# Loads of k and v for the last two batches: k through SyncE's queue, v through GpSimd's, fewer and larger issues for batch 18

## The chip, the cores and the metric

The kernel runs on one core of a Trainium2 chip. The metric is the device time of one execution in microseconds (us); the median of three runs before the change is 207.99 us (207.58 to 208.32).

## What is computed

The reference chains two parts. The first is a recurrence over the sequence, per batch and head; the second is a feed-forward network with squared ReLU on its output.

```python
# q, k, v: [4 batches, 8 heads, 768 steps, 64]; gamma[h] = 1 - 2**(-5-h); scale = 1/8
for t in range(768):
    state = gamma * state + outer(k[:, :, t], v[:, :, t])      # [4, 8, 64, 64]
    y[:, :, t] = scale * q[:, :, t] @ state
x = y laid out as [3072 tokens, 512]
h = maximum(x @ w_in, 0)          # w_in  [512, 2048]
out = (h * h) @ w_out             # w_out [2048, 512], out float32
```

## The kernel before, in words

**Chunks and blocks.** The recurrence is computed in chunks of 128 steps: six chunks for each of four batches, numbered 0 to 23. Chunks 6 to 11, 12 to 17 and 18 to 23 are the second, third and fourth batch. For each chunk TensorE (PE) makes scores (k against q), which VectorE masks, the state (k against v, added up over the chunks of a batch), and outputs (v against the masked scores, plus the state against q). The outputs become x of the feed-forward part. Its work goes in blocks of four chunks and then of two; the second matrix product is done with seven products of half size in place of eight, from sums that VectorE prepares.

**Where the order comes from.** The order is written out by hand. The feed-forward part is a list of pieces of TensorE work; the place number n counts them, from 4 upward. `put(place, what, ...)` hangs a step of the recurrence, a load or a store in front of that place. So the program order on every engine, and on SyncE's and GpSimd's queues, follows from the places, and each engine takes its instructions in that order. A chunk takes eight places in the later part of the kernel, which is about 7.5 us of TensorE's time.

**The half form (chunks 8 to 23), `attend2`.** The chunk's last step, the outputs, has place d. In front of it stand, for an even chunk, the scaling of q by VectorE (`scale_q`, two steps) and a transpose of q by a DMA on SyncE's queue (`dma_transpose_q`, L425); for every chunk

- `cast_k2` (L658): GpSimd casts k from the staged float32 tile into `ks_bdp`, in two halves of 64 partitions; there are two such tiles, taken in turn;
- `transpose_k2` (L681): a transposing DMA on SyncE's queue writes `kT` from `ks_bdp`; there are two kT tiles;
- `scale_v2`: VectorE scales v by the table `kf2` (L667), and GpSimd copies the result into `v_bd`, in two halves (L675);
- `scores2` (L697, five places ahead of d): TensorE multiplies kT with the transposed q, and VectorE masks (L704);
- `state2` (L724) and `outputs2` (L746, L753).

For chunks 12 to 23, k is cast at d - 18, transposed at d - 13, and v scaled and copied at d - 9. d is 57, 62, and then 70, 78, 86 and so on.

**Loads of q.** One load on SyncE's queue brings q for two chunks (512 KB, L105).

**Loads of k and v for the half form, `batch_loads`.** It is a generator: each `next` issues one load (L147) of some chunks of one head's k or v into 64 partitions of a staged tile. Four pairs of heads and two halves make eight issues for a group of chunks. Batch "8" (chunks 8 to 11, the last four of the second batch) is loaded four chunks at a time on SyncE's queue, batch 12 (chunks 12 to 17) and batch 18 (18 to 23) three at a time on GpSimd's queue. `places` says at which place each issue stands. The first half of batch 12's k goes into a tile that held sums of the feed-forward part.

**Other steps around it.** `pack_constants` makes lng2, a mask and, in its second step, the table `kf2` (two VectorE operations, L202 and L203, and one on ScalarE, L284); the steps stand at places 22 and 38. The stores of the feed-forward part (L886, L888) go through SyncE's queue too.

Of the kernel before, what the change touches and what calls it, by code (L numbers as in the profile page):

```python
# [28 lines left out]
def kernel(  # L29
# [9 lines left out]
    nc = tc.nc  # L39
# [87 lines left out]
    def stage_tile(size):  # L127
        t = stage.tile([P, 2 * NCH * NPAIR * D], FP32, name="stage")
        return t[:, 0:size]
# [3 lines left out]
    def batch_loads(m, name, size):  # L133


        b, i = chunks[m]
        src, to = (k, raw_k) if name == "k" else (v, raw_v)
        t = kept_tiles.pop((m, name), None)
        if t is None:
            t = stage_tile(2 * NCH * NPAIR * D)  # L140
        t = t.rearrange("s (p w d) -> s p w d", p=NPAIR, d=D)
        for j in range(NCH - i):
            to[m + j] = t[:, :, 2 * j : 2 * j + 2].rearrange("s p u d -> s u p d")
        for w in range(0, NCH - i, size):
            for hh, rows in enumerate(halves):
                for p in range(NPAIR):
                    (nc.sync if m == 8 else nc.gpsimd).dma_start(  # L147
                        t[rows, p, 2 * w : 2 * (w + size)],
                        src[b, 2 * p + hh, (i + w) * C : (i + w + size) * C].rearrange(
                            "(w s) d -> s w d", s=64  # L150
                        ),
                    )
                    yield
# [110 lines left out]
    def pack_constants():  # L264
        lng2 = const.tile([P, 2, NPAIR], FP32)
        for hh, rows in enumerate(halves):
            for p in range(NPAIR):
                nc.gpsimd.memset(lng2[rows, :, p : p + 1], float(np.log(gammas[2 * p + hh])))
        logs = lng2.rearrange("s u p -> s (u p)")
        scaled = exponents([[C, NCH], [C // 2, 2], [0, NPAIR]], 1, "ex_k2", logs, halves)  # L270
        nc.gpsimd.memset(cmask2[:], 0.0)
        for rows in halves:
            nc.gpsimd.affine_select(
                out=cmask2[rows],
                in_=cmask2[rows],
                compare_op=ALU.is_gt,
                fill=1.0,
                base=0,
                pattern=[[-1, 2], [-2, C // 4]],
                channel_multiplier=1,  # L280
            )
        yield
        ex = scaled()
        nc.scalar.activation(kf2.rearrange("s i u p -> s i (u p)"), ex[:], AF.Exp, scale=-1.0)  # L284
        yield
# [73 lines left out]
    at = {m: {} for m in range(NCHUNK)}  # L359
# [303 lines left out]
    def scale_v2(m):  # L663
        b, i = chunks[m]
        vn = raw_v.pop(m)
        v2 = v2pool.tile([P, 2 * NPAIR, D], BF16, name="v2")
        nc.vector.tensor_tensor(  # L667
            out=v2.rearrange("s (u p) d -> s u p d", u=2),
            in0=vn,
            in1=kf2[:, i, :, :, None].to_broadcast([P, 2, NPAIR, D]),  # L670
            op=ALU.mult,
        )
        v_bd = v_bd2s[m % 2]
        for hh, rows in enumerate(halves):
            nc.gpsimd.tensor_copy(v_bd[rows, :, hh, :], v2[rows])  # L675
        at[m].update(v2=v2, v_bd=v_bd)

    def transpose_k2(m):
        a = at[m]
# [535 lines left out]
    def put(place, what, *args):  # L1215
        parts.setdefault(place, []).append((what, args))
# [17 lines left out]
    def attend2(m, d, before, q_at, qturn_at, k_at, turn_at, v_at):  # L1234
        if m % 2 == 0:
            put(q_at, scale_q, m, 0)
            put(q_at + 1, scale_q, m, 1)
            put(qturn_at, dma_transpose_q, m)
        put(k_at, cast_k2, m)
        put(v_at, scale_v2, m)  # L1240
        put(turn_at, transpose_k2, m)
        put(max(d - 6, before), state2, m, 0)
        put(d - 5, scores2, m)
        put(d - 3, state2, m, 1)
        put(d, outputs2, m)
# [40 lines left out]
        put(place, early_store, tb, which)  # L1286
    packed = pack_constants()
    put(22, next, packed)
    put(38, next, packed)
    for j, t in enumerate(ks_bd2s + v_bd2s + [s_bds[2]]):  # L1290
        for hh in range(2):
            put(24 + j, zero_off_diagonal, t, hh)
# [7 lines left out]
    for m, d in zip(range(PACK_FROM, NCHUNK), done):  # L1300
        attend2(m, d, done[m - PACK_FROM - 1] if m > PACK_FROM else 0,
                *ahead.get(m, (d - 19, d - 16, d - 18, d - 13, d - 9)))
        if m >= 12 and m % 2 == 0:
            put(d - 33, load_q, m)
    places = {
        (8, "k"): [23, 23, 24, 24, 25, 32, 32, 33],
        (8, "v"): [33, 33, 34, 34, 35, 35, 36, 36],
        (12, "k"): [49, 50, 51, 52, 53, 54, 55, 56] + [74 + j for j in range(8)],
        (12, "v"): [58, 59, 60, 61, 62, 64, 65, 66] + [82 + j for j in range(8)],
        (18, "k"): [92 + 4 * j // 3 for j in range(8)] + [117 + 4 * j // 3 for j in range(8)],  # L1310
        (18, "v"): [103 + 4 * j // 3 for j in range(8)] + [128 + 4 * j // 3 for j in range(8)],
    }
    for (m, name), at_places in places.items():
        loads = batch_loads(m, name, 4 if m == 8 else 3)
        for place in at_places:
            put(place, next, loads)

# [53 lines left out]
```

## Time and profile before

| what | value |
|---|---|
| median of three runs | 207.99 us (207.58 to 208.32) |
| the profiled execution | 208.36 us, span 206.6 us |
| granted TensorE clock, mean | 0.998 |
| DMA queues | SyncE's: q1, hardware_dynamic; GpSimd's: q0, software_dynamic |
| k and v for batches 12 and 18 | 32 + 32 issues on GpSimd's queue, 96 KB each, 4.5 and 4.9 us median to landing |
| kT | 16 transposes on SyncE's queue, 4.9 us median to landing (3.1 to 9.5) |
| HBM | 27.26 MB read, 6.29 MB written |

The page gives, for each engine, busy time and its share of the span. PE is TensorE's matrix work, PEld its loading of weights, DVE is VectorE, ACT is ScalarE, POOL is GpSimd, SP is SyncE and SPq its queue of instructions. L147 is line 147 of the kernel. A group's line names what it writes and reads as out<-in, with buffer numbers left out. Waits are put down to what came last. The chain of waits goes back from the last instruction to what released it, step by step; its lines give a start, a duration and the work. "Issue to landing" of a DMA is from the start of its issue to the last of its completion marks.

### The profile page before, as it was taken

The numbers are of one execution on the slowest core, as the hardware profiler recorded it, in microseconds if no ns is written. First come the engines' busy times: TensorE is split into PE (matmuls) and PEld (weight loads), VectorE is DVE, ScalarE is ACT, GpSimd is POOL, SyncE is SP. The second block draws the span as 40 slices with busy tenths as digits, with TensorE's granted clock in tenths as the row PEclk, the third lists the DMA queues.
The fourth block names the chain that finished last, engine by engine and source line by source line (L and its number), as shares of the span: only waits on it lengthen the run. The fifth ranks groups of instructions, "written<-read, shape, count | busy, mean of one in ns | idle before, by whom it ended". The sixth has DMA issues, their size and how long they took to land.

```text
span 206.6 us, 5855 instructions
## 1 busy us (share of the span) xinstructions
PE 196.7 (95%) x2373; PEld 165.2 (80%) x2373; DVE 152.9 (74%) x305; ACT 135.6 (66%) x276; POOL 112.1 (54%) x198
## 2 busy tenths in 40 slices
PE   5889999999999999999999899999999999999993
PEld 1457644876888998789989699999989999898883
DVE  4687899498885678589697588598697797474374
ACT  8375885677943666693794595793785786874730
POOL 5332549823230768975999788779986226100000
PEclk9999999999999999999999999999999999999999
DMA  6999999999999999899699998799897551300202
GB/s 160 290 313 379 310 268 247 205 203 239 238 169 174 240 292 134 149 289 185 174 200 180 221 225 176 190 197 158 217 201 156 137 105 38 119 0 3 102 0 102
DMA packets 70730, 38.12 MB, mean 185 GB/s; under 512 B 43952, under 2 KB 64688, under 8 KB 70704
## 3 DMA queue, kind: packets, MB, share of 16 engines
q1 hardware_dynamic: 65520, 29.37, 68.4%
q0 software_dynamic: 5184, 8.39, 19.2%
q8 instruction: 18, 0.29, 0.6%
q14 instruction: 8, 0.07, 0.1%
HBM read 27.26 MB, written 6.29 MB: 162 GB/s over the span
## 4 chain that ended last, share of the span: by engine, by line
PE 69%; DMA 17%; POOL 4%; DVE 4%; ACT 2%; issue 1%; SPq 0%; DVEq 0%; ACTq 0%
PE psf L803 28%; PE psf L837 12%; PE tp L837 8%; DMA kT<-ks_bdp 7%; PE psf L1096 6%; DMA stage<-in_moe_w_in_dram 4%; DMA w_out_bf<-in_moe_w_out_dram 3%; PE psf L1002 3%; DMA kn<-in_k_dram 3%; POOL stage L147 2%; PE st L697 2%; POOL ks_bdp L658 2%; PE y L753 1%; PE y L746 1%; PE c_ps L724 1%
## 5 line engine op out<-in xcount | busy, mean ns | idle before, releaser
L803 PE MATMUL psf<-xt,w_in_bf 128*128 128x256 bf16 (+2 forms) x880 | 92.5, 259 | 0.4 <-DVE w_in_bf L336 0.3
L803 PEld LDWEIGHTS <-w_in_bf 128*128 128x128 bf16 x880 | 70.9, 98 | 11.2 <-DVE w_in_bf L336 0.7
L812 ACT ACTIVATE h<-psf 128x512 bf16<-128x512 f32 x96 | 56.2, 595 | 20.5 <-PE psf L803 20.0
L774 DVE TENSOR_TENSOR h<-h 128x512 bf16<-128x512 bf16 x72 | 31.8, 458 | 14.8 <-ACT h L812 14.6
L658 POOL CAST ks_bdp<-stage 64x512 bf16<-64x512 f32 x32 | 25.6, 799 | 20.6 <-issue 12.1
L675 POOL COPY v_bd<-v 64x512 bf16<-64x512 bf16 x32 | 20.6, 642 | 23.4 <-DVE v L667 22.2
L837 PEld LDWEIGHTS <-h 128*128 128x128 bf16 x288 | 26.3, 98 | 3.3 <-DVE h L774 0.6
L833 DVE TENSOR_TENSOR osb<-psf,u 128x256 f32<-128x256 f32 x34 | 13.7, 422 | 17.1 <-ACT u L878 9.9
L147 POOL DMA_DIRECT2D stage<-in_k_dram x32 | 21.0, 662 | 0.0
L147 POOL DMA_DIRECT2D stage<-in_v_dram x32 | 21.0, 662 | 0.0
L760 ACT ACTIVATE xt<-y 128x512 bf16<-128x512 f32 x16 | 12.0, 748 | 8.8 <-PE y L753 8.8
L366 DVE TENSOR_TENSOR qs<-qn,qf 128x512 bf16<-128x512 f32 x22 | 16.6, 758 | 1.1 <-DMA qn<-in_q_dram 1.1
L837 PEld LDWEIGHTS <-k_bd 128*128 128x128 bf16 x144 | 13.7, 98 | 1.8 <-issue 0.2
L772 ACT ACTIVATE h<-h 128x512 bf16<-128x512 bf16 x24 | 14.6, 626 | 0.5
L667 DVE TENSOR_TENSOR v<-stage,kf 128x512 bf16<-128x512 f32 x16 | 13.4, 838 | 0.0
L733 ACT ACTIVATE s_bd<-c_ps 64x256 bf16<-64x256 f32 x29 | 10.6, 367 | 3.4 <-PE c_ps L724 3.3
L704 DVE TENSOR_TENSOR pt<-st,cmask 128x512 bf16<-128x512 f32 x16 | 11.0, 687 | 2.4 <-PE st L697 1.9
L734 ACT ACTIVATE s_bd<-c_ps 64x256 bf16<-64x256 f32 x29 | 11.0, 378 | 0.4
L837 PE MATMUL tp<-w_out_bf,h 128*128 128x256 bf16 x72 | 11.2, 273 | 0.0
L334 POOL CAST w_in_bf<-stage 128x256 bf16<-128x256 f32 x14 | 6.1, 465 | 9.2 <-DMA stage<-in_moe_w_in_dram 9.2
L837 PE MATMUL psf<-w_sum,h 128*128 128x256 bf16 x72 | 10.8, 273 | 0.0
L833 DVE TENSOR_TENSOR k_bd<-h 128x512 bf16<-128x512 bf16 x18 | 10.4, 576 | 0.3
(146 smaller groups left out, 328.7 us busy)
## 6 DMA issues: line engine op xcount, KB each, us to landing
qn<-in_q_dram SPq DMA_DIRECT2D x12, 512.0 KB, 7.0
out_dram<-osb SPq DMA_DIRECT2D x23, 256.0 KB, 3.3
stage<-in_k_dram POOLq DMA_DIRECT2D x32, 96.0 KB, 4.5
stage<-in_v_dram POOLq DMA_DIRECT2D x32, 96.0 KB, 4.9
stage<-in_moe_w_in_dram SPq DMA_DIRECT2D x4, 512.0 KB, 6.9
stage<-in_moe_w_in_dram SPq DMA_DIRECT2D x2, 1024.0 KB, 10.9
w_out_bf<-in_moe_w_out_dram POOLq DMA_DIRECT2D x4, 512.0 KB, 9.5
kn<-in_k_dram SPq DMA_DIRECT2D x2, 512.0 KB, 6.4
```

Of the source, the lines that this page charges most:

```text
L147: (nc.sync if m == 8 else nc.gpsimd).dma_start(t[rows, p, 2 * w : 2 * (w + size)], src[b, 2 * p + hh, (i + w) * C : (i + w + size) * C].re ...
L366: engine.tensor_tensor(out=out, in0=by, in1=table[:, :, None].to_broadcast([P, H, D]), op=ALU.mult)
L658: nc.gpsimd.tensor_copy(ks[rows, :, hh, :].rearrange("s (u p) d -> s u p d", u=2), kn[rows])
L667: nc.vector.tensor_tensor(out=v2.rearrange("s (u p) d -> s u p d", u=2), in0=vn, in1=kf2[:, i, :, :, None].to_broadcast([P, 2, NPAIR, D]), ...
L675: nc.gpsimd.tensor_copy(v_bd[rows, :, hh, :], v2[rows])
L772: nc.scalar.activation(hv, hv, AF.Square)
L774: nc.vector.tensor_mul(hv, hv, hv)
L803: nc.tensor.matmul(hp, lhsT=w_in_bf[g][:, cb, fq * 128 : (fq + 1) * 128], rhs=xts[tb][:, cb, cols], start=(cb == 0), stop=(cb == NCB - 1),)
L812: nc.scalar.activation(hv, hp[:], AF.Relu)
L833: nc.vector.tensor_tensor(out=out, in0=in0, in1=in1, op=op)
L837: nc.tensor.matmul(to, lhsT=left[:, j], rhs=right(j) if callable(right) else right[:, j], start=(start and j == 0), stop=(stop and j == NF ...
L1096: nc.tensor.matmul(to[:], lhsT=left(j), rhs=right(j), start=(start and j == 0), stop=(j == NFB // 2 - 1), skip_group_check=True,)
```

## The change

- The loads of k for batches 12 and 18 are issued on SyncE's queue; those of v stay on GpSimd's.
- Batch 18 is loaded six chunks at a time: eight issues for k and eight for v in place of sixteen each.
- The places of the loads of batches 12 and 18 are new. Batch 12: k at 58 to 65 (before 49 to 56) and 74 to 81 (as before), v at 60 to 67 and 82 to 89. Batch 18: k at every second place from 92 to 106, v from 100 to 114; before, both were loaded in two parts between 92 and 138.
- GpSimd's copies of the scaled v are a step of their own, `copy_v2`, one place behind the scaling.
- The second step of `pack_constants` stands at place 42 instead of 38.

In the built program SyncE's order from chunk 10 on becomes: kT 10, five loads of k, kT 11, three loads, two stores, q, qT 12, kT 12, seven loads, kT 13, one load, two stores, q, qT 14, kT 14, three loads (192 KB each from here), kT 15, one load, two stores with one load behind them, q, qT 16, two loads, kT 16, one load, kT 17, and from there as before.

```diff
-                    (nc.sync if m == 8 else nc.gpsimd).dma_start(
+                    (nc.sync if m == 8 or name == "k" else nc.gpsimd).dma_start(
...
             op=ALU.mult,
         )
+        at[m]["v2"] = v2
+
+    def copy_v2(m):
         v_bd = v_bd2s[m % 2]
         for hh, rows in enumerate(halves):
-            nc.gpsimd.tensor_copy(v_bd[rows, :, hh, :], v2[rows])
-        at[m].update(v2=v2, v_bd=v_bd)
+            nc.gpsimd.tensor_copy(v_bd[rows, :, hh, :], at[m]["v2"][rows])
+        at[m]["v_bd"] = v_bd
...
         put(v_at, scale_v2, m)
+        put(v_at + 1, copy_v2, m)
...
-    put(38, next, packed)
+    put(42, next, packed)
...
-        (12, "k"): [49, 50, 51, 52, 53, 54, 55, 56] + [74 + j for j in range(8)],
-        (12, "v"): [58, 59, 60, 61, 62, 64, 65, 66] + [82 + j for j in range(8)],
-        (18, "k"): [92 + 4 * j // 3 for j in range(8)] + [117 + 4 * j // 3 for j in range(8)],
-        (18, "v"): [103 + 4 * j // 3 for j in range(8)] + [128 + 4 * j // 3 for j in range(8)],
+        (12, "k"): [58 + j for j in range(8)] + [74 + j for j in range(8)],
+        (12, "v"): [60 + j for j in range(8)] + [82 + j for j in range(8)],
+        (18, "k"): [92 + 2 * j for j in range(8)],
+        (18, "v"): [100 + 2 * j for j in range(8)],
     }
     for (m, name), at_places in places.items():
-        loads = batch_loads(m, name, 4 if m == 8 else 3)
+        loads = batch_loads(m, name, {8: 4, 12: 3, 18: 6}[m])
```

## Prediction

> **What bounds the kernel now.** I read the page's busy times first, then who TensorE (PE) waited for from 66 us to 200 us, then the chain that ended last, then SyncE's queue in time.
>
> ```profile
> PE 196.7 (95%) x2373; PEld 165.2 (80%) x2373; DVE 152.9 (74%) x305; ACT 135.6 (66%) x276; POOL 112.1 (54%) x198
> ```
> ```profile
> PE st L697 <- DMA kT<-ks_bdp: 1.5, 2, 1.0
> ```
>
> PE is busy for 95% of the span, and in the stretch that the change touches it waits twice, both times for a transposed k (kT) that its scores (L697) read. By the distance between the starts of neighbouring matmuls, less the usual 0.11 us, the two cost 0.62 us at 84.2 and 1.18 us at 115.5: 1.8 us, all that the change can win there. The chain shows what stood before them:
>
> ```profile
> 75.54 1.26 POOL stage L147 x2
> 76.84 0.79 POOL ks_bdp L658
> 77.68 0.70 POOL ks_bdp L658
> 78.40 5.75 DMA kT<-ks_bdp
> 84.20 0.41 PE st L697 x8
> ...
> 101.39 1.97 POOL stage L147 x3
> 103.40 1.02 POOL ks_bdp L658
> 104.47 0.96 POOL ks_bdp L658
> 105.43 0.53 POOL stage L147
> 105.96 9.46 DMA kT<-ks_bdp
> 115.47 0.41 PE st L697 x8
> ```
>
> Load issues (L147) on GpSimd (POOL), then the cast of k, then the transposing DMA, then PE. The first wait is kT of chunk 10, the second of chunk 14. Note 5.75 and 9.46 us for the same DMA: at 173 us, with nothing beside it, one takes 3.1 (issue to landing). The rest is queue. Per chunk, first score against landing, the margins are small for even chunks (8: 1.2; 10: 0; 12: 0.2; 14: 0; 16: 130.45 - 128.45 = 2.0; 18: 1.6; 20: 1.4 us) and 4.5 to 8.6 for the odd ones: an even kT is issued right behind a load of q (512 KB) and the transpose of q.
>
> **The change, part by part.** Durations are from the one profiled execution (span 206.6, its own time 208.36, which is 0.37 above the median of 207.99).
>
> ```profile
> L147 POOL DMA_DIRECT2D stage<-in_k_dram x32: 656/662/684, 69.1 to 145.6; - x32
> L147 POOL DMA_DIRECT2D stage<-in_v_dram x32: 656/662/672, 79.6 to 154.4; - x32
> L147 SPq DMA_DIRECT2D stage<-in_k_dram x8: 611/634/1563, 47.2 to 54.6; - x8
> ```
>
> *GpSimd is relieved.* 64 issues of 0.66 us (42.4 us) become 24: 16 of the old size and 8 of twice the chunks. No row has such an issue; it lies between 0.66 and two of them, 1.32, and I take 1.0, nearer the w_out issue of 512 KB at 0.75. POOL loses about 42.4 - 10.6 - 8 = 24 us. It is idle nearly half the time, so that counts only at the two waits. Chunk 10: the two issues (1.31) ahead of the cast go, its kT is issued 1.3 us earlier and PE needs 0.6: -0.62 (0 if the queue eats it). Chunk 14: the cast comes earlier, but SyncE issues qT of chunk 14 from 103.97 to 105.80, and kT only behind it, at 105.96: the issue gains 0.16, and the queue decides the rest. I take -0.2; the ends are -1.18 and +1.0 (below).
>
> *SyncE's queue gets k.* 16 loads of 96 KB (batch 12) and 8 of 192 KB (batch 18). SyncE issues and queue land in order: the loads of batch 8 landed in the order of issue, qn, qT and kT behind them. So every k load issued ahead of a kT is in its way, while before it went through another queue.
>
> ```profile
> q1 hardware_dynamic: 65520, 29.37, 68.4%
> q0 software_dynamic: 5184, 8.39, 19.2%
> ```
>
> Price of a load there: the 16 loads of batch 8 (128 KB each, SyncE's, from 47 us on) landed one behind the other at 0.736 us on average over 13 gaps (shortest 0.47; the last eight 0.79). By size that is 0.55 us for 96 KB and 1.10 for 192 KB (ends 0.71 and 1.19). On GpSimd's queue, four 96 KB loads issued from 115.1 landed 0.35 apart. The queue lines say why they differ: q0 moved 1.6 KB per packet, q1 0.45.
>
> The Trainium skill ("DMA: Bandwidth & Descriptors", section Queues, rings and completion order) says that each DMA engine keeps the order of a ring and takes turns between queues, packet by packet. It speaks against this change: k left its own ring for that of the transposes; the landings above agree on the order.
>
> Batch 12, first half: five loads behind kT 10, three behind kT 11, ahead of 88 us; kT 11 has 4.5 us of margin, and five loads are 2.8. kT 12 is issued after they landed: nothing. Second half: seven stand behind kT 12, ahead of kT 13 (8.6 us of margin), and fall between the landings of kT 13 (99.90) and qn 16 (109.55), where the queue's own work is two stores (0.77 each) and qn (1.90), so 6.2 us are free for 8 x 0.55 = 4.4, up to 4.8. If kT 13 (1.2 to 2.4) is pushed in there too, it is over by 1.0: that is the +1.0 at chunk 14.
>
> Batch 18: three loads go behind kT 14, one behind kT 15, one ahead of qn 18, two between qT 16 and kT 16: seven between kT 14 and kT 16. SyncE there, before:
>
> ```profile
> 118.11 0.33 SPq L888 DMA_DIRECT2D out_dram<-osb  x1
> 118.49 1.11 SPq L105 DMA_DIRECT2D qn<-in_q_dram  x1
> 120.66 1.30 SPq L425 DMA_TRANSPOSE qT<-qs  x1
> 122.14 7.87 SPq L681 DMA_TRANSPOSE kT<-ks_bdp  x2
> ```
>
> From kT 14's landing (115.42) to kT 16's (128.45) the landings are kT 15 +1.92, store +0.77, store +4.16, qn +1.90, qT +1.25, kT +3.03. Only the second store has a hole: 4.16 - 0.77 = 3.4 us. Seven loads at 1.10 are 7.7; less the hole and the margin of 2.0 the score waits 2.3 us (ends: 5.0 - 5.4, so none, and 8.3 - 5.4 = 2.9). SyncE's own issue time (0.63 to 1.27 each, no row has this size; 0.8 taken) delays kT 16's issue by 0.6 to 2.5 us past the 1.3 that SyncE idled; it lies under the queue, kT 16 having taken 6.3 where 3.1 is bare. Behind kT 16 stands one load; then both queues are empty of loads 20 us earlier than before, so the kTs of 18 to 23 come sooner and win nothing, PE waiting for none now.
>
> Added waits: in the built order each SyncE issue waits for the landing of the issue eight before it. kT 16 then waits for the load behind kT 15, which is ahead of it in the queue anyway; behind it stand only kT 17 and stores.
>
> *v's half-form table and copies later.* The table (two small VectorE operations, 0.48 and 0.65 us, and one of 0.24 on ScalarE) goes behind two masks of scores; v of chunk 8 needs it at 67.1, over 4 us later. The copies of v go one place later, behind casts of k; the outputs read them 4.5 us or more after the copies ended, a cast being 0.7. Nothing; PE's gaps from 58 to 64 us bound the table at 0.4 either way.
>
> Sum: -0.62 - 0.2 + 2.3 = +1.5 us, 209.9 in the profiled execution, **209.5** beside the median.
>
> **The rivals.**
> *A. Loads cost the same on either queue, faster.* At 2 x 0.35 = 0.70 the seven loads are 4.9 us, under the 5.4 of hole and margin: kT 16 is in time, the waits at chunks 10 and 14 go, 207.99 - 1.8 = 206.2. For it: the shortest gap (0.47) gives the same, and bytes are unchanged. Against: 0.736 over 13 gaps. It decides below 0.77 us a load. The Trainium skill's same page (Issuing engines are not separate DMA queues) states that the issuing engine saves only issue time; by that rule this rival holds, and 0.35 against 0.55 us for 96 KB speaks against it.
> *B. A worse backlog.* The hole is not filled, since loads behind kT 14 land before it: only 1.3 of the 3.4 serve, loads cost 1.19, chunk 14 loses its 1.0: 8.3 - 1.3 - 2.0 + 1.0 - 0.62 = +5.4, 213.4.
> *C. Both cancel.* At 0.9 us a load chunk 16 waits 6.3 - 5.4 = 0.9, the gain is 0.8: 208.0.
>
> **How the numbers follow.** 0.3% (0.62 us) is about what a measurement can tell from no change. Forecast 0.49 (208.6 to 211), A 0.28, B 0.11, C 0.12. Faster 0.28, within 0.3% 0.12, slower 0.49 + 0.11 = 0.60. The range reaches from A to beyond the forecast's upper end (0.62 from load price, 1.2 from chunk 14): 206.2 to 212.2.
>
> **What would show it.** Right: no wait at 84, PE waiting 1 to 3 us for kT of chunk 16 near 130, its landing over 8 us after issue, k loads of 192 KB landing 1.1 us apart, POOL near 88 us busy. Wrong: no wait at chunk 16 (A), or waits at odd chunks, which would mean that SyncE's queue is behind throughout (B).

## The result, and the profile after

The changed kernel takes 219.61 us in the median of six runs (215.9 to 222.34); the kernel before, run beside it, 208.04 us (207.46 to 208.78). The ratio is 1.0441, 95% interval 1.0363 to 1.052. The change makes the kernel slower by about 9 us; 209.5 was forecast, so sign and place are as forecast and the size is not. The profiled execution took 221.4 us (span 219.6); it is one of the longer ones, which the ratio leaves out, so the 13 us found in it below are more than the 9 of the ratio.

The page of the changed kernel: busy time of the engines, the granted clock of TensorE in 40 slices of 5.5 us, and the two DMA queues (packets, MB, share of 16 engines' span).

```profile
PE 197.2 (90%) x2369; PEld 166.0 (76%) x2373; DVE 153.2 (70%) x305; ACT 135.8 (62%) x276; POOL 86.4 (39%) x158
...
PEclk9789999999999999999999997579999999999999
...
q1 hardware_dynamic: 78192, 32.52, 73.5%
q0 software_dynamic: 3392, 5.24, 13.0%
```

PE does the same work as before (197.2 us against 196.7) in a longer span: nearly all of the added time was waited. GpSimd was relieved as planned, 86.4 us against 112.1. 3.15 MB moved from q0 to q1. And at one place, slices 25 to 27 (131.8 to 148.2 us), the clock falls to 7, 5 and 7 tenths.

Whom PE waited for between 60 and 215 us (us in total, times, longest); this line is the whole answer:

```profile
PE st L700 <- DMA kT<-ks_bdp: 12.5, 2, 10.6
```

Two waits as before, both for a kT, the longest 10.6 us where it was 1.0. (The profile counts such a wait from the end of the matmul before it; by the starts of neighbouring matmuls, as in the prediction, it is some 0.16 us longer: 10.77.) The lines of the code have moved by three (scores L697, now L700; `transpose_k2` L681, now L684; `copy_v2` L678). The chain of the changed kernel tells what was in front of them:

```profile
110.07 6.00 DMA kT<-ks_bdp
116.08 0.05 issue
116.12 0.41 PE st L700 x8
...
127.53 14.29 DMA kT<-ks_bdp
141.82 0.04 issue
141.87 0.61 PE st L700 x8
142.48 1.71 PE psf L806 x8
```

First the kT of chunk 14, then that of chunk 16: 14.29 us from issue to landing, for a transfer that takes 3.1 alone. Behind it eight matmuls of L806 last 1.71 us, where eight of them took 0.87 in front of the wait: the clock, 0.50 from 142 to 145 us. What the 10.6 us and the clock cost is seen best by setting the start of each chunk's first score beside that of before:

| chunk | 8 | 10 | 12 | 13 | 14 | 15 | 16 | 17 | 18 | 23 |
|---|---|---|---|---|---|---|---|---|---|---|
| before, us | 71.79 | 84.20 | 99.23 | 108.55 | 115.47 | 124.71 | 130.45 | 139.68 | 145.30 | 184.35 |
| after, us | 72.46 | 84.26 | 99.11 | 108.32 | 116.12 | 125.36 | 141.87 | 152.72 | 158.35 | 197.40 |
| lag, us | +0.67 | +0.06 | -0.12 | -0.23 | +0.65 | +0.65 | +11.42 | +13.04 | +13.05 | +13.05 |

The lag falls by 0.61 at chunk 10 (its wait is gone), rises by 0.88 at chunk 14, by 10.77 at chunk 16 and by 1.62 between 16 and 17, and then stays: 13.05 is the difference of the two spans (219.6 - 206.6). One wait and the slow clock behind it are 12.4 of 13.0 us.

SyncE's queue of instructions in the changed kernel (start, duration of the issues, the DMA):

```profile
120.20 1.26 SPq L105 DMA_DIRECT2D qn<-in_q_dram  x1
121.55 4.46 SPq L425 DMA_TRANSPOSE qT<-qs  x1
126.06 1.36 SPq L147 DMA_DIRECT2D stage<-in_k_dram  x2
127.53 5.59 SPq L684 DMA_TRANSPOSE kT<-ks_bdp  x1
```

Before, qT 16 was issued at 120.66 in 1.30 us and kT 16 at 122.14. Now kT 16's issue starts 5.4 us later: the issue of qT ahead of it starts 0.9 us later and lasts 3.2 longer, and the issues of two loads (1.36) stand between. It then lands 14.29 instead of 6.32 us after. What landed between kT 14 (116.08) and kT 16 (141.82), by the completion marks: of batch 18's k, on SyncE's queue, seven loads (117.45, 118.73, 119.83, 122.71, 125.17, 134.16, 136.66); of its v, on GpSimd's queue, seven loads as well (126.67, 130.30, 131.58, 132.86, 138.83, 140.18, 141.43). The gaps inside the runs of three are 1.1 to 1.4 us on either queue. Before, the same stretch held eleven loads of half that size, all on GpSimd's queue, and lasted 13.03 us; now it lasts 25.74. By the records of the DMA packets at least fifteen were in flight at every moment of these 25.74 us, on 16 DMA engines.

### The profile page after: what moved, and what is told of

Same layout as the page of the kernel before. It is cut to its first block, busy times and chain, and to the rows that moved or that the text cites. A ratio compares the mean times of both kernels' runs of the same rounds, so it can differ in the third digit from the quotient of the medians.

```text
span 219.6 us, 5836 instructions
## 1 busy us (share of the span) xinstructions
PE 197.2 (90%) x2369; PEld 166.0 (76%) x2373; DVE 153.2 (70%) x305; ACT 135.8 (62%) x276; POOL 86.4 (39%) x158
## 4 chain that ended last, share of the span: by engine, by line
PE 70%; DMA 18%; DVE 3%; issue 2%; ACT 2%; POOL 2%; SPq 1%; DVEq 0%
PE psf L806 31%; PE psf L840 11%; DMA kT<-ks_bdp 9%; PE tp L840 8%; PE psf L1099 6%; DMA stage<-in_moe_w_in_dram 4%; DMA w_out_bf<-in_moe_w_out_dram 4%; PE psf L1005 3%; DMA qn<-in_q_dram 2%; PE st L700 2%; PE y L756 1%; PE y L749 1%; PE c_ps L727 1%; POOL stage L147 1%; PE y L347 1%
## 5 line engine op out<-in xcount | busy, mean ns | idle before, releaser
L806 PE MATMUL psf<-xt,w_in_bf 128*128 128x256 bf16 (+2 forms) x878 | 93.1, 260 | 0.7 <-DVE w_in_bf L336 0.6
L806 PEld LDWEIGHTS <-w_in_bf 128*128 128x128 bf16 x880 | 71.3, 98 | 11.8 <-DVE w_in_bf L336 1.2
L678 POOL COPY v_bd<-v 64x512 bf16<-64x512 bf16 x32 | 20.5, 639 | 26.2 <-DVE v L667 20.1
L836 DVE TENSOR_TENSOR osb<-psf,u 128x256 f32<-128x256 f32 x34 | 13.7, 421 | 17.6 <-ACT u L881 9.0
L366 DVE TENSOR_TENSOR qs<-qn,qf 128x512 bf16<-128x512 f32 x22 | 17.4, 796 | 1.0 <-DMA qn<-in_q_dram 1.0
L700 PE MATMUL st<-qT,kT 128*128 128x64 bf16 x128 | 6.6, 196 | 12.5 <-DMA kT<-ks_bdp 12.5
L147 POOL DMA_DIRECT2D stage<-in_v_dram x24 | 16.5, 695 | 0.0
L700 PEld LDWEIGHTS <-kT 128*128 128x128 bf16 x128 | 5.7, 100 | 13.4 <-DMA kT<-ks_bdp 13.1
L736 ACT ACTIVATE s_bd<-c_ps 64x256 bf16<-64x256 f32 x29 | 10.6, 367 | 3.4 <-PE c_ps L727 3.3
L836 DVE TENSOR_TENSOR k_bd<-h 128x512 bf16<-128x512 bf16 x18 | 10.6, 590 | 0.3
L840 PE MATMUL psf<-w_sum,h 128*128 128x256 bf16 x72 | 10.8, 273 | 0.0
```

The lines of the kernel that those rows point to most:

```text
L147: (nc.sync if m == 8 or name == "k" else nc.gpsimd).dma_start(t[rows, p, 2 * w : 2 * (w + size)], src[b, 2 * p + hh, (i + w) * C : (i + w ...
L366: engine.tensor_tensor(out=out, in0=by, in1=table[:, :, None].to_broadcast([P, H, D]), op=ALU.mult)
L678: nc.gpsimd.tensor_copy(v_bd[rows, :, hh, :], at[m]["v2"][rows])
L700: nc.tensor.matmul(st[:, c, :], lhsT=kT[:, c, :], rhs=half_of(a["qT"], p, u), start=True, stop=True,)
L806: nc.tensor.matmul(hp, lhsT=w_in_bf[g][:, cb, fq * 128 : (fq + 1) * 128], rhs=xts[tb][:, cb, cols], start=(cb == 0), stop=(cb == NCB - 1),)
L836: nc.vector.tensor_tensor(out=out, in0=in0, in1=in1, op=op)
```

## The experiments

The theory on record counts SyncE's own queue: a load of k there costs 1.10 us, and the loads of v on GpSimd's queue cost what they did (below: **ring**). The rivals: the larger loads of v running beside are what delays the transposes (**traffic**); and, after the first runs, that a load costs a kT the same on whichever queue it is, so that loads of both are to be counted together (**bytes**). Every kernel was run beside the kernel before, which took 209.5, 209.6 and 209.2 us (medians) beside e1 to e4, e5 to e8 and e9 to e12, so ratios are compared. A lag is against the profiled execution of before, by starts of scores, as in the table above.

**e1: the small edits alone.** The kernel before with `copy_v2` and the table's step at 42.

```diff
...
+        put(v_at + 1, copy_v2, m)
...
-    put(38, next, packed)
+    put(42, next, packed)
```

> The kernel before with the two small edits alone: copies of v one place later, the half form's table at place 42. All theories: no part of the loss is here, 208.0 within 0.6 us. If it is over 209, the order on GpSimd or VectorE matters after all and both theories below are short of something.

210.44 us, ratio 1.0039 (0.9988 to 1.0089): no difference that can be told. The table and the copies are not it. (The profiled execution, 213.64 us, is the longest of its ten; in it chunk 14 waits 3.5 us. Waits differ between executions, see e7 and e12.)

**e2: v of batch 18 as before.** The changed kernel, but v in loads of 96 KB at the old places.

```diff
-        (18, "v"): [100 + 2 * j for j in range(8)],
+        (18, "v"): [103 + 4 * j // 3 for j in range(8)] + [128 + 4 * j // 3 for j in range(8)],
...
-        loads = batch_loads(m, name, {8: 4, 12: 3, 18: 6}[m])
+        loads = batch_loads(m, name, 3 if (m, name) == (18, "v") else {8: 4, 12: 3, 18: 6}[m])
```

> The changed kernel with v of batch 18 as before: three chunks an issue, the old places, 16 issues on GpSimd's queue; k of batch 18 stays on SyncE's queue. Theory 'ring' (the prediction's: seven k loads stand in SyncE's queue between kT 14 and kT 16 and make kT 16 late by themselves): PE's wait for kT 16 stays near the 10.6 us of the changed kernel, time 215 to 217. Theory 'traffic' (the eight 192 KB loads of v, which landed 1.3 us apart on GpSimd's queue, hold SyncE's queue still while they last, 10.4 us in all): the wait falls to 3 us or less, time 208 to 211.

214.53 us, ratio 1.0255 (1.0176 to 1.0334): by the ratios some two fifths of the loss go, and the time lies between the two expectations. Whom PE waited for, 60 to 215 us:

```profile
PE st L700 <- DMA kT<-ks_bdp: 7.5, 3, 4.1
```

By starts, 1.44 us at chunk 12, 4.22 at chunk 14 and 2.30 at chunk 16: with the seven loads of k in SyncE's queue and v as it was, chunk 16 waits what the prediction gave it (in part by luck, see below), and not the 10.6 that was expected of ring here. kT 16 lands 19.0 us behind kT 14 instead of 25.7: these 6.8 us go with v's larger and earlier loads. Another 1.7 of the difference in the wait come from PE, which a slow clock made that much later.

**e3: k of batch 18 through GpSimd.** The changed kernel with the other half undone: only batch 12's k on SyncE's queue.

```diff
-                    (nc.sync if m == 8 or name == "k" else nc.gpsimd).dma_start(
+                    (nc.sync if m == 8 or (m, name) == (12, "k") else nc.gpsimd).dma_start(
```

> The changed kernel with k of batch 18 on GpSimd's queue, places and size of an issue as in the changed kernel (16 issues of 192 KB there). Theory 'ring': nothing stands ahead of kT 16 but q, the wait at chunk 16 goes, time 208.5 or less. Theory 'traffic': 16 software loads at 1.3 us are 21 us in which SyncE's queue is held back, the wait at chunk 16 stays at 8 us or more, time 215 or more.

Four times from 213.56 to 225.97 us, median 217.09, no interval. In the profiled execution (216.07 us) chunk 16 hardly waits (0.2 us), but chunk 17 does for 2.62 and chunk 18 for 1.44: with no load of batch 18 in SyncE's queue, kT 17 still takes 13.69 us from issue to landing (132.19 to 145.88), and sixteen loads are served on the other queue between 118.2 and 148.2 us. Ring has no room for that; the wait moved by one chunk, as the loads did. Neither expectation came true as written: the time is over ring's 208.5, and the wait that traffic expected, 8 us or more, is not at chunk 16. SyncE's queue there:

```profile
138.57 10.90 SPq L425 DMA_TRANSPOSE qT<-qs  x1
```

**e4: batch 12's part alone.** The kernel before, with k of batch 12 on SyncE's queue and k and v of batch 12 at the new places.

```diff
-                    (nc.sync if m == 8 else nc.gpsimd).dma_start(
+                    (nc.sync if m == 8 or (m, name) == (12, "k") else nc.gpsimd).dma_start(
...
```

> The kernel before with the part for batch 12 alone: its k on SyncE's queue, its k and v at the new places; batch 18, the copies and the table as before. Both theories: chunk 10's wait (0.6 us) goes, chunk 14's (1.2) changes to between 0 and 2.1 (2.1 in the changed kernel), no wait of over 1 us at chunk 16: 206.8 to 209.

211.35 us, ratio 1.0097 (1.0057 to 1.0137). Chunk 10's wait is gone (0.62 won), chunk 12 waits 1.06 and chunk 14 2.43 us. Batch 12 alone loses about 2 us; 206.8 to 209 was expected.

**e5: v of batch 18 on SyncE's queue too.** The changed kernel; nothing of batch 18 is left on GpSimd's queue.

```diff
-                    (nc.sync if m == 8 or name == "k" else nc.gpsimd).dma_start(
+                    (nc.sync if m == 8 or name == "k" or m == 18 else nc.gpsimd).dma_start(
```

> The changed kernel with v of batch 18 on SyncE's queue too (192 KB an issue, same places): nothing of batch 18 goes through GpSimd's queue, and ten loads in place of seven stand between kT 14 and kT 16. Theory 'ring' (what stands ahead of kT 16 in SyncE's queue makes the wait, GpSimd's traffic adds little): three loads more, the wait at chunk 16 grows from 10.6 to about 14 us, time 219 or more. Theory 'traffic' (SyncE's queue stands still while GpSimd's has 192 KB loads to move): without them the ten loads cost 10 x 1.10 less 5.4 of hole and margin, a wait of 4 to 7 us, time 211 to 215.

216.06 us, ratio 1.0329 (1.0249 to 1.0408). Ten loads now stand ahead of kT 16 in its own queue, and chunk 16 waits 3.08 us, not 10.8: three more loads in the ring, and still fewer served in all (10 against 14). Ring expected about 14 us of wait, traffic 4 to 7.

**e6: k of batch 18 in two bunches behind kTs.** The changed kernel.

```diff
-        (18, "k"): [92 + 2 * j for j in range(8)],
+        (18, "k"): [97] * 4 + [105] * 4,
```

> The changed kernel with other places for k of batch 18: four loads right behind kT 15 and four right behind kT 16, so none between q and kT 16 and four in place of seven between kT 14 and kT 16. v of batch 18 stays in 192 KB issues on GpSimd's queue. Theory 'ring': four loads are 4.4 us, under hole and margin, no wait at chunk 16, time 208 to 210 (chunk 14's wait stays). Theory 'traffic': the first four v loads, issued from 120.7 to 124.8, still hold qT 16 and kT 16 until about 132, a wait of 1.5 to 4 us at chunk 16; time 210 to 214.

215.33 us, ratio 1.0287 (1.019 to 1.0384). kT 16 is issued 3.5 us earlier than in the changed kernel, at 124.07, and lands at 134.59; chunk 16 waits 3.24 us, chunk 14 2.38 and chunk 18 0.5. Ring expected no wait at chunk 16, traffic 1.5 to 4 us, and 210 to 214 in all.

**e7 and e12: another order, nothing on SyncE's queue.** The kernel before, with its loads moved behind the casts that two kTs wait for. e12 is the same kernel once more.

```diff
-        (12, "k"): [49, 50, 51, 52, 53, 54, 55, 56] + [74 + j for j in range(8)],
-        (12, "v"): [58, 59, 60, 61, 62, 64, 65, 66] + [82 + j for j in range(8)],
-        (18, "k"): [92 + 4 * j // 3 for j in range(8)] + [117 + 4 * j // 3 for j in range(8)],
+        (12, "k"): [49, 50, 51, 52, 56, 56, 56, 56] + [74 + j for j in range(8)],
+        (12, "v"): [58, 59, 60, 61, 62, 64, 65, 66] + [90 + j // 2 for j in range(8)],
+        (18, "k"): [94 + 4 * j // 3 for j in range(8)] + [117 + 4 * j // 3 for j in range(8)],
```

> The kernel before with its loads on GpSimd's queue, some places moved: two loads of k of batch 12 behind the cast of chunk 10 in place of ahead of it, the second half of v of batch 12 behind kT 14 (places 90 to 93 in place of 82 to 89), the first of k of batch 18 two places later. Theory 'traffic': the software loads that ran beside qT 14 and kT 14 are gone, the cast of 10 is 1.3 us earlier, so both waits of the kernel before (0.6 and 1.2) go: 1 to 2 us under before. Theory 'ring' (kT 14 is late for what stands ahead of it in SyncE's own queue): only chunk 10's 0.6 goes.

> The kernel of e7_loads_behind_casts unchanged, beside e11 on the same chip: again 0.3 to 1.2% under the kernel before.

e7: 208.3 us, ratio 0.9923 (0.9876 to 0.997); e12: 209.29 us, ratio 1.0019 (0.9975 to 1.0063). Whom PE waited for in e7, and then in e12:

```profile
PE st L697 <- DMA kT<-ks_bdp: 0.6, 1, 0.6
```
```profile
PE st L697 <- DMA kT<-ks_bdp: 4.0, 2, 3.0
```

The same program waited 0.6 us in one execution and 4.0 in another (in e12 the longest at chunk 16, 3.2 by starts). The gain of e7 was not found again; whether this order is worth anything stays open.

**e8: the first half of batch 12's k alone on SyncE's queue.** The kernel before.

```diff
-                    (nc.sync if m == 8 else nc.gpsimd).dma_start(
+                    (nc.sync if m == 8 or (m, name, w) == (12, "k", 0) else nc.gpsimd).dma_start(
...
-        (12, "k"): [49, 50, 51, 52, 53, 54, 55, 56] + [74 + j for j in range(8)],
+        (12, "k"): [58 + j for j in range(8)] + [74 + j for j in range(8)],
```

> The kernel before with only the first half of batch 12's k on SyncE's queue (eight loads of 96 KB, places 58 to 65); the second half and all else stay on GpSimd's. Both theories: chunk 10's wait (0.6 us) goes. If the second half's seven loads behind kT 12 are what cost batch 12's part 1% (by the queue ahead of qT 14, whose issue took 4.5 us in place of 1.8), the time is 0.3 to 0.6 us under before; if it is the first half, it is 1 us or more over before with a wait at chunk 12.

208.97 us, ratio 0.9996 (0.9952 to 1.0041). The waits at chunks 10 and 14 are gone and one of 2.08 us at chunk 12 has come: the price of the first half is paid at chunk 12. It does not follow that the wait at chunk 14 in e4 belongs to the second half alone. There qT 14's issue takes 4.48 us and here 1.34, but kT 14 lands only 0.8 us earlier than in e4 (116.20 against 117.03), and PE comes to chunk 14 2.3 us later, after the wait at 12 and 1.5 us lost behind it to the clock. An estimate from these: with PE as early as in e4, chunk 14 would have waited 1.6 us here too.

**e9: v of batch 18 later.** The changed kernel, with the same seven loads of k ahead of kT 16 and the same sizes, but v moved behind.

```diff
-        (18, "v"): [100 + 2 * j for j in range(8)],
+        (18, "v"): [107 + 3 * j // 2 for j in range(8)],
```

> The changed kernel with v of batch 18 later (places 107 to 117 in place of 100 to 114), still eight issues of 192 KB on GpSimd's queue; SyncE's queue is exactly that of the changed kernel, seven k loads ahead of kT 16. Theory 'bytes' (formed from the runs so far: what counts is how many loads are served between the landings of kT 14 and kT 16, on either queue, at 1.2 us for 192 KB; 5.5 such loads fit before, and 2.0 us of margin above that): seven loads, 1.8 us over, under the margin, so a wait of 0 to 1 us at chunk 16. Theory 'ring': seven loads in SyncE's queue make the wait by themselves, 2.3 us by the prediction's sum; and if GpSimd's traffic has nothing to do with it, near 10. Time 210.5 to 212.5 with the waits at chunks 12 and 14 that batch 12's part brings.

Four times from 214.43 to 222.38 us, median 220.2, no interval. Whom PE waited for, 60 to 215 us:

```profile
PE st L700 <- DMA kT<-ks_bdp: 6.3, 3, 4.9
PE c_ps L727 <- DVE v L667: 3.5, 1, 3.5
```

The kT waits are 1.31 us at chunk 12 and 5.02 at chunk 14; at chunk 16 there is none. SyncE's queue holds what it held in the changed kernel, and kT 16 takes 6.05 us instead of 14.29. One content of the ring, and a wait of 10.8 us or none (1.6 if PE had not lost 2.6 us to its clock just before): ring cannot give both, and bytes does (fourteen loads served between the two kTs there, eight here). The time isn't won, since v itself is late now: its last load landed at 155.59, and the state (L727) waited 3.5 us for it; 210.5 to 212.5 had been expected. Loads of v that are in the way of k in one place are missing in another.

**e10: batch 18's part alone.** The changed kernel with batch 12 as before, all of it on GpSimd's queue.

```diff
-                    (nc.sync if m == 8 or name == "k" else nc.gpsimd).dma_start(
+                    (nc.sync if m == 8 or (m, name) == (18, "k") else nc.gpsimd).dma_start(
...
```

> The changed kernel with batch 12 as in the kernel before (k and v on GpSimd's queue at the old places); batch 18, copies and table as changed. Theory 'bytes': 14 loads are served between kT 14 and kT 16 as in the changed kernel, a wait of 6 to 11 us at chunk 16; batch 12's 2 us are gone, so 212 to 216. If the wait is under 4 us, it needed batch 12's loads on SyncE's queue too (the backlog that they leave).

223.46 us, ratio 1.0658 (1.0569 to 1.0746). Whom PE waited for, 60 to 215 us:

```profile
PE st L700 <- DMA kT<-ks_bdp: 15.8, 3, 12.1
```

Chunk 16 waits 12.3 us by starts, with fifteen loads of batch 18 and two of 96 KB served between the two kTs. Batch 18's part makes the long wait by itself; batch 12's isn't needed for it. The time is not what was expected: 212 to 216 was, since batch 12's loss is undone, and the kernel is slower than the changed one (the two intervals do not meet). In the profiled execution chunk 10 waits 2.5 us and 1.3 follow to the clock, and the wait at 16 is longer than the 6 to 11 expected; why the loads of batch 18 cost more here is not settled.

**e11: v of batch 12 later still.** The kernel of e7, with

```diff
-        (12, "v"): [58, 59, 60, 61, 62, 64, 65, 66] + [90 + j // 2 for j in range(8)],
-        (18, "k"): [94 + 4 * j // 3 for j in range(8)] + [117 + 4 * j // 3 for j in range(8)],
+        (12, "v"): [58, 59, 60, 61, 62, 64, 65, 66] + [92] * 8,
+        (18, "k"): [97 + j for j in range(8)] + [117 + 4 * j // 3 for j in range(8)],
```

> The kernel of e7_loads_behind_casts with the second half of v of batch 12 later still (all eight issues at place 92, behind the cast of chunk 15) and the first eight of k of batch 18 at places 97 to 104. Theory 'bytes': no load is served beside kT 14, its last 0.6 us of wait goes, 206 or a little under, 0.3 to 0.6 us under e7. If v of chunk 15 comes too late for VectorE's scaling at 120 us, that is given back.

210.98 us, ratio 1.0082 (1.0033 to 1.013); 206 or a little under was expected. PE waits for no kT at all, but for v and what follows from it:

```profile
PE tp L837 <- DVE h L774: 1.3, 1, 1.3
PE c_ps L724 <- DVE v L667: 1.0, 1, 1.0
```

**All runs together.** For each kernel's profiled execution: what was served between the landings of kT 14 and kT 16, in loads of 192 KB (one of 96 KB is a half), the time between these landings, and the wait at chunk 16.

| kernel | on SyncE's queue | on GpSimd's | us between kT 14 and kT 16 | wait at chunk 16, us |
|---|---|---|---|---|
| before | 0 | 5.5 | 13.0 | 0 |
| e1 | 0 | 4.5 | 14.0 | 0 |
| e4 | 0 | 5 | 13.2 | 0 |
| e8 | 0 | 5.5 | 14.1 | 0 |
| e3 | 0 | 6 | 16.7 | 0.2 |
| e11 | 0 | 6 | 17.7 | 0 |
| e7 | 0 | 6.5 | 15.0 | 0 |
| e6 | 4 | 4 | 18.2 | 3.2 |
| e12 | 0 | 8 | 19.8 | 3.2 |
| e9 | 7 | 1 | 16.6 | 0 |
| e2 | 7 | 1.5 | 19.0 | 2.3 |
| e5 | 10 | 0 | 19.7 | 3.1 |
| changed | 7 | 7 | 25.7 | 10.8 |
| e10 | 7 | 9 | 27.3 | 12.3 |

Each row is one execution, and one program can differ between two: e7 and e12 are the same kernel, and 4.8 us apart. A straight fit through the fourteen rows gives 7.6 us, and 1.21 for a load on SyncE's queue (standard error 0.11), and 1.35 for one on GpSimd's (0.15); no row is off by more than 2.1 us. The two prices agree within their errors. The count of both queues together explains 92% of the spread, the count on SyncE's queue alone 43%. A stretch that is longer for another reason also has more landings in it, so the fit alone is no proof. What stands beside it is e9 against the changed kernel, where v's places are all that was changed: six loads fewer in the stretch, and 9.1 us less. Neither ring nor traffic alone stands: 2.3 us are left without v's new loads (e2), 3.1 without any load on the other queue (e5), and 13.7 us from issue to landing without any load of batch 18 on SyncE's (kT 17 in e3). Bytes forecast that e9's wait would be 0 to 1 us; e10's wait (6 to 11) it put too low, and the times of the whole kernel it missed in e9, e10 and e11. The last column follows from the one before it: chunk 16's scores come 15.0 us behind kT 14's landing when nothing holds PE up (13.0 and the margin of 2.0). For e10 that gives 27.3 - 15.0 = 12.3, for the changed kernel 10.7, for e6 3.2. In e2 and e5 PE itself lost 1.7 us to its clock between chunks 14 and 15, which leaves 2.3 and 3.1; in e9 2.6 us, more than the 1.6 that the landing leaves, so there is no wait. In e11 and e12 kT 14 landed 3.4 and 1.2 us ahead of its scores, which comes off too.

The Trainium skill ("DMA: Bandwidth & Descriptors", Issuing engines are not separate DMA queues) says that transfers interleave on the same 16 engines whoever started them, and that another issuer saves only issue time. The runs agree: 1.21 against 1.35 us.

## Why the prediction was wrong

*Chunk 10: 0.62 won.* Right. kT 10 was issued at 77.67 instead of 78.40, although PE was 0.67 us later at that point, and landed at 81.55; the lag fell by 0.61.

*Chunk 14: -0.2.* Wrong in sign and inside its ends: +0.88. The cast was earlier, as said, but qT 14's issue took 4.57 us where 1.83 were assumed unchanged, and kT 14 was issued behind it, at 110.07 instead of 105.96. In e4, where of batch 18 nothing is changed, it takes 4.48, and in e8, without the second half of batch 12's k on SyncE's queue, 1.34: that half did not fit into free time of the queue. How much of the wait at chunk 14 is its doing stays open (e8).

*Batch 12, first half: nothing.* Wrong where it can be seen. Chunk 12, which waits for nothing in the kernel before, waits 0.6 to 2.1 us in seven of the eight profiled kernels that have this half on SyncE's queue (e2 to e6, e8, e9). The eighth is the changed kernel, and there kT 12 landed only 0.05 us ahead of its scores.

*Batch 18: the price of a load, 1.10 us (ends 0.71 and 1.19).* Nearly right: 1.1 to 1.3 us between landings, 1.21 in the fit. That the loads stand ahead of kT 16 and are seven was right as well, and with v as before (e2) the wait is the forecast 2.3. That figure is luck in part: the stretch from kT 14 to kT 16 grew there by 5.9 us and not by 4.3, and 1.7 of it do not show, because PE lost them to its clock.

*Batch 18: "only the second store has a hole", and v left out.* This is **the step that failed**. The prediction took 3.4 us of idle time in SyncE's queue as room for k, and counted nothing for GpSimd's queue, where eight large loads of v had been put into the same 25 us. That hole was no idle time of the DMA engines. It lies between 118.1 and 121.5 us, and for its first half they were serving GpSimd's loads; from 119.8 on they were serving SyncE's own store and load of q. The queues in the kernel before from 118.0 to 119.75 (packets, MB, share of 16 engines):

```profile
q0 software_dynamic: 126, 0.26, 97.5%
q1 hardware_dynamic: 2, 0.00, 1.3%
```

0.26 MB in 1.75 us are 0.66 us for 96 KB, 1.32 for 192: the price of the fit once more, read from GpSimd's queue alone. GpSimd's loads were spread over the places 92 to 137 before the change, and only 5.5 units of 192 KB fell between kT 14 and kT 16. Its sum for the stretch was 7 x 1.10 - 3.4 = 4.3 us more; measured are 12.7. Without the hole it is 7.7; at the fit's price of k 8.5; and with v, (7 - 5.5) x 1.35 = 2.0, it is 10.5. The other 2.2 are the scatter of the fit: before lies 1.9 below the line and the changed kernel 0.3 above it. Of the 12.7 only the margin of 2.0 is hidden, and PE pays the rest.

*"It lies under the queue" (SyncE's issue time).* Too simple: the issue itself grows with the queue. Each transpose's issue is longer when the queue ahead is full, 4.46 us for qT 16 and 5.59 for kT 16 against 1.3 and 2.1. These issues end about when what is ahead in the queue lands: in the changed kernel kT 16's issue ends at 133.12, and qT 16 landed at 133.22; before, kT 16's ended at 124.25, with the load of q for 18 landing at 124.17. So the late issue is the backlog seen from the other side, not a second price. That is read from coincidences of times; no run tests it.

*Not in the sum at all: the clock.* 1.62 us behind the long wait, at a granted clock of 0.50 until 145 us.

*The table and the copies of v: nothing.* Right within what e1 can tell.

*Rivals.* A (loads cost the same on either queue, faster) had the rule right and the outcome wrong: with one price, moving k saves nothing at the engines, and what counts is how much is pulled into the stretch. The prediction spoke against that rule with 0.35 us for 96 KB on GpSimd's queue; where these loads stood in a backlog, four landed 0.50 to 0.68 apart (113.37, 114.05, 114.67, 115.16 in the changed kernel). The four that gave 0.35 are those of the fence above: nearly all of their packets had been moved by 119.8 us, before the first of them was marked as landed at 120.62, so the distance of their marks is no price, and the packet sizes explain no difference where there is none. B (the hole not filled) was the closest, 213.4, and it too left v at nothing. What is still open: the wait differs between executions of one program (e7 and e12), so 10.8 us is the size in the profiled one, and the six times from 215.9 to 222.34 say that it is less in others.

## What to carry to other kernels

Before loads are moved from one DMA queue to another, count the bytes of all queues that are served between two transfers that the critical engine needs, and price them alike: here 1.2 to 1.35 us for 192 KB on either queue. A gap in one queue's landings is not free time as long as another queue has work. Pulling loads ahead of their need (here batch 18's, issued up to 28 places sooner) puts them ahead of the transfers that are needed next, and pushing them back (e9, e11) makes them late themselves.

## What the runs showed of the hardware that was not expected

*A short wait of PE can cost most of its own length again in clock, or nothing.* Two runs waited the same at chunk 14, e5 (2.36 us) and e6 (2.38). The columns behind the busy times are the granted clock, the DMA share and GB/s.

```profile
113.38:116.79 3.41, 1.21 (x18) 0.88 (x16) 0.76 (x2) 1.46 (x4) 0.28 (x1) 1.00 1.27 183
116.79:120.20 3.41, 3.41 (x18) 2.44 (x17) 1.12 (x3) 1.23 (x2) 0.00 (x0) 0.50 1.35 170
```
```profile
111.68:115.09 3.41, 2.52 (x38) 2.07 (x36) 1.37 (x4) 2.37 (x5) 1.89 (x3) 1.00 1.20 215
115.09:118.50 3.41, 2.09 (x25) 1.90 (x26) 1.02 (x2) 0.74 (x2) 0.00 (x0) 1.00 1.34 196
```

After its wait e5 ran 3.41 us at half the clock and lost 1.67 us; e6 lost nothing. By the lags, such a loss (1.6 to 2.6 us) followed all eight waits for a kT of 3 us or more in these traces, and four of the nine between 2.0 and 2.7 us (1.3 to 1.7 us). What decides is how the wait falls on a grid: in these traces the granted clock changes only at multiples of 3.41 us from its first record, and the fences show grid windows. e5's wait lies in one window (3.41 - 1.21 = 2.20 us without a matmul); e6's is cut in two (0.89 and 1.32). Between 20 and 200 us the fourteen traces have 13 windows at full clock with 1.91 us or more without a matmul, and the clock was 0.50 in the window behind each of them; behind the 22 with 0.82 to 1.86 us it never was. The Trainium skill ("TensorE: Matmul & The Clock Gate", Part 1: The HAM clock gate) has the clock at one half after an idle window of about 3.4 us that runs freely. The half (0.50) and the length of the window agree; a window idle for 1.91 of its 3.41 us was enough.

*The issue of a transposing DMA on SyncE is no fixed price.* 1.23 us in an empty queue; up to 6.84 us for kT 16 in e10 and 10.90 for qT 18 in e3, with sixteen loads on the other queue.

*A load issue of GpSimd hardly grows with the load.* 0.66 us for 96 KB, 0.75 for 192 KB (1.0 was taken).
